# A fused attention, MLP and expert kernel on one core: splits, conversions and products moved between VectorE, ScalarE, GpSimd and TensorE

## The chip, the cores and the metric

The kernel runs on one core of a Trainium2 chip. Of its engines five matter here: TensorE (PE; its weight loads are listed apart as PEld), VectorE (DVE), ScalarE (ACT), GpSimd (POOL) and the queue of SyncE (SP) that issues the DMAs. Each engine takes its own instructions in order; semaphores tie them together. The metric is the device time of one execution in microseconds (us), the median of the runs shown.

## The reference

Three layers run one after the other. Inputs come in float32, the MLP's weights in float64.

```python
# 1. attention with random features, per head: 2 batches, 8 heads, 576 tokens, dimension 64, m = 128 features
q_s, k_s = q * scale, k * scale                      # scale = 64 ** -0.25
proj = x @ omega.T                                   # for k and for q
phi(x) = exp(proj - |x|^2/2 - rowmax(...)) / sqrt(m)
out = (phi(q) @ (phi(k).T @ v)) / (phi(q) @ sum_s phi(k) + 1e-6)
# 2. MLP on 1152 tokens, d_model 512, d_ff 2048
h = x @ w_in ;  g = h * tanh(softplus(h)) ;  y = g @ w_out
# 3. experts: 8, capacity 288
logits = y @ w_gate ; expert = argmax ; gate = softmax(logits)[expert]
position of a token = count of earlier tokens of its expert ; keep = position < capacity
out[i] = keep * gate * relu(y[i] @ w1[e]) @ w2[e]
```

## The kernel before

**Split numbers.** Most matmuls are done in float32r, a rounded form of float32. Each operand is cut into a high part (the rounded number) and a low part (the rest): `split_hi_lo` issues one copy or cast for the high part and one subtraction for the low part, each on an engine that the caller names. `mm3` then issues three matmuls (high x high, lines L67 to L69).

**Stage 1, attention (0 to 94 us).** Two heads make a pair, eight pairs in all. A pair has four or five tiles of 128 tokens. `beat` issues the work of one tile: `proj` (the projection, into a bank of PSUM `pj`), `phi` (on DVE the row maximum `mx`, L233, then `nm`, the maximum times minus the scale, L237; on ACT the exponential `e`, L242, and for q the shifted projection, L245), and beside it the previous pair's products: transposes `qt`, the sums `kvp`, and denominators and numerators `den` and `num` of two pairs. `split` cuts the k and q of a whole pair (1024 or 1280 columns) on POOL, two pairs ahead. The result x is split into `xh` and `xl`. A Tile scheduler orders this stage.

**Stage 2, first MLP layer (94 to 220.7 us).** The order here is the order of the program on each engine. The 2048 columns of `w_in` come in 16 chunks j. For each chunk `hmm(j, c)` makes a third c of the tokens: 12 matmuls of 384 columns into one of three banks `pj`. `hout` copies the bank to `g` (L430), on DVE for c = 0 and 1, on ACT for most c = 2; the bank is free for the third product after it only then. `convert` turns float64 bits to float32 in three DVE steps of 512 columns (L110, L112, L114), for `w_in` (`wi` to `wif`), for `w_out` (`wo` to `wl`) and for a transposed copy of `w_out` that the host lays out (`wt` to `woT`). `w_in`'s two parts `wih` and `wil` are made on POOL (L59, L63). The activation `mish` takes two chunks at a time in alternating ScalarE tables: in an even chunk a table load, tanh, sigmoid, tanh, sigmoid, and in an odd one a table load and two logarithms (L465 to L469, 1152 columns each); the product g times tanh follows on POOL (L470). `wgate_u` and `wgate_s` make w_out x w_gate out of `woT` (tiles `wu`, `us`, `ws`), from which `logits` gets the routing's logits `lg`.

**Stage 3, y of the first 288 tokens, and routing (220.7 to 262.1 us).** `ymm(ps0, j)` is 12 matmuls of 288 columns for each chunk of `w_out`, whose parts `whi`, `wl` and those of `g`, `gh`, are made two or three chunks ahead. Beside it run the last activations, the logits and `route0` to `route2`, a chain of small DVE steps and three matmuls `rp` with running sums `cu`.

**Stage 4 (262.1 to 349.9 us).** y of a second group of tokens, two experts' two layers each, and the output.

In stage 1, `phi` before the change:

```python
V.tensor_reduce(out=mx, in_=pv, op=ALU.max, axis=AX.X)
...
V.tensor_tensor(out=nm, in0=mx, in1=sgn, op=ALU.mult)
shift = p < 2 and t in (1, 3)
if shift:
    V.tensor_tensor(out=e[:, 2:4, :], in0=pv[:, 2:4, :], in1=mx[:, 2:4, None].to_broadcast([128, 2, M]), op=ALU.subtract)
for j in range(2):
    S.activation(out=e[:, j, :], in_=pv[:, j, :], func=AF.Exp, scale=SCALE, bias=nm[:, j : j + 1])
```

Of the kernel before, what the change touches and what calls it, by code (L numbers as in the profile page):

```python
# [32 lines left out]
def performer_mish_moe(  # L33
# [7 lines left out]
    w_outT: bass.AP,  # L41
# [12 lines left out]
    def split_hi_lo(src, hi, lo, eng_hi="act", eng_lo="pool"):  # L54
        """hi = src rounded to float32r, lo = src - hi (exact in float32r)."""
        if eng_hi == "act":
            S.copy(out=hi, in_=src)  # L57
        elif eng_hi == "pool":
            P.tensor_scalar(out=hi, in0=src, scalar1=1.0, scalar2=0.0, op0=ALU.mult, op1=ALU.add)  # L59
        else:  # L60
            V.tensor_copy(out=hi, in_=src)
        e = P if eng_lo == "pool" else V
        e.tensor_tensor(out=lo, in0=src, in1=hi.bitcast(F32), op=ALU.subtract)  # L63

    def mm3(o, lh, ll, rh, rl, start, stop):
        """o += (lh + ll)^T (rh + rl), without the product of the low parts' last bits."""
# [4 lines left out]
    # ---------------------------------------------------------------- constants  # L71
# [12 lines left out]
    # the eight PSUM banks: pj x 3, qt x 2, b0, b1, b2  # L84
# [13 lines left out]
    # w_in chunks for the float64 conversion: in flight while the attention runs  # L98
    fhl = tc.alloc_tile_pool(name="fhl", bufs=3)
# [7 lines left out]
    def conv64(t, dst):  # L107
        """float64 bit patterns to float32 (all bits that fit) in three steps; zero, or in float32's normal range."""
# [7 lines left out]
    win, wo, woT, raw = {}, {}, {}, {}  # L116

    def fetch(kind, j):
        src = dict(wi=w_in, wo=w_out, wt=w_outT)[kind]
# [27 lines left out]
    def finish(*gens):  # L147
        """what is left of each generator"""
# [4 lines left out]
    def steps(*gens):  # L153
        """four steps of each generator, in turn"""
# [3 lines left out]
    def hmm(j, c):  # L158
        """x @ w_in for a chunk of d_ff and a third of the tokens"""
# [7 lines left out]
    # ---------------------------------------------------------------- attention  # L167
    # phi's term |x|^2/2 is the same for all features of a row, so it cancels
    # against the row maximum; 1/sqrt(m) is carried by EPS.
    with ExitStack() as c2:  # L170
        a1 = c2.enter_context(tc.tile_pool(name="a1", bufs=1))
        omf = a1.tile([128, 2 * M], F32, name="omf")
        nc.sync.dma_start(out=omf, in_=omt)
# [5 lines left out]
        # the tensor engine's clock rises while the first operands are on their way  # L179
# [3 lines left out]
        for _ in range(8):  # L183
            T.matmul(out=wp, lhsT=wb[:, 0:128], rhs=wb, start=True, stop=True)
        split_hi_lo(omf, omh, oml, "dve", "dve")
# [21 lines left out]
        def halves(p):  # L207
            """the engines of the pieces' high and low parts"""
            return (("act", "dve"),) * 3 if p == 0 else (("act", "pool"),) * 2 if p == 1 else (("pool", "pool"),)

        def split(p):
# [3 lines left out]
            for c, e in zip(pieces(p), halves(p)):  # L215
# [3 lines left out]
        def proj(p, t):  # L219
            d = st[p]  # L220
            # the first pairs find the other banks empty
            first = {(0, 3): "b1", (1, 0): "b2", (1, 3): "b1", (1, 4): "b2"}
            d["p", t] = ps = bank(first.get((p, t), "pj"), "pj")
            for i in range(2):
                s = slice(256 * t + 128 * i, 256 * t + 128 * i + 128)
                mm3(ps[:, i * 256 : i * 256 + 256], d["h"][:, s], d["l"][:, s], omh, oml, True, True)

        def phi(p, t):
            """phi's exponents of a tile of tokens: exp for k, the shifted projection for q"""
            d = st[p]  # L230
            pv = d.pop(("p", t)).rearrange("p (g m) -> p g m", m=M)
            mx = a3.tile([128, 4], F32, name="mx", tag=f"mx{t}")
# [3 lines left out]
            nm = a3.tile([128, 4], F32, name="nm", tag=f"nm{t}")  # L236
            V.tensor_tensor(out=nm, in0=mx, in1=sgn, op=ALU.mult)  # L237
            shift = p < 2 and t in (1, 3)
            if shift:
                V.tensor_tensor(out=e[:, 2:4, :], in0=pv[:, 2:4, :], in1=mx[:, 2:4, None].to_broadcast([128, 2, M]), op=ALU.subtract)  # L240
            for j in range(2):
                S.activation(out=e[:, j, :], in_=pv[:, j, :], func=AF.Exp, scale=SCALE, bias=nm[:, j : j + 1])  # L242
# [4 lines left out]
        def kvm(p, h):  # L247
            """kv and, in the last column, the sum of phi(k) over the tokens: one accumulation for two pairs"""
# [9 lines left out]
        def kvc(u):  # L258
            """kv, and the sum of phi(k) in 32 equal columns"""
# [7 lines left out]
        def qtr(p, h):  # L267
# [21 lines left out]
        def den(u):  # L289
            """-1 / (the denominators), the same in the 32 rows of a head: a first value and a step of Newton's"""  # L290
# [17 lines left out]
        def num(u, k, last=False):  # L308
            """x^T for one half of the four heads' dimensions"""
# [12 lines left out]
            split_hi_lo(x, xh[:, e + k, c], xl[:, e + k, c], *(("act", "dve") if last else ("pool", "pool")))  # L322
# [27 lines left out]
        def beat(i, t, *pe):  # L350
            """a tile of pair i beside the tensor engine's other work, and the rest of what the last beat began"""
# [648 lines left out]
```

## Time and profile before

| | us |
|---|---|
| median of 3 runs (351.24, 352.63, 354.53) | 352.63 |
| span of the profiled execution, first to last instruction | 349.9 |
| median less that span | 2.7 |
| PE busy | 314.4 (90%) |
| DVE busy | 265.7 (76%) |
| ACT busy | 191.4 (55%) |
| POOL busy | 153.2 (44%) |

Matmuls overlap each other, so a busy PE is not yet a PE at its pace: the time from one matmul's start to the next one's is what it costs. The granted clock is the share of TensorE's full clock (2.4 GHz) that a stretch got; 0.50 is the lower of its two levels (1.2 GHz).

### The profile page before, as it was taken

The numbers are of one execution on the slowest core, as the hardware profiler recorded it, in microseconds if no ns is written. First come the engines' busy times: TensorE is split into PE (matmuls) and PEld (weight loads), VectorE is DVE, ScalarE is ACT, GpSimd is POOL, SyncE is SP. The second block draws the span as 40 slices with busy tenths as digits, with TensorE's granted clock in tenths as the row PEclk, the third lists the DMA queues.
The fourth block names the chain that finished last, engine by engine and source line by source line (L and its number), as shares of the span: only waits on it lengthen the run. The fifth ranks groups of instructions, "written<-read, shape, count | busy, mean of one in ns | idle before, by whom it ended". The sixth has DMA issues, their size and how long they took to land.

```text
span 349.9 us, 5915 instructions
## 1 busy us (share of the span) xinstructions
PE 314.4 (90%) x2159; PEld 281.1 (80%) x2160; DVE 265.7 (76%) x453; ACT 191.4 (55%) x375; POOL 153.2 (44%) x107
## 2 busy tenths in 40 slices
PE   8869988999999959699879989999599999999992
PEld 5758666767899959569875888677599999999992
DVE  5986999974789999987999999998935447324321
ACT  4657566697128736566554849584324663515411
POOL 2866693504064837556463711376610443241400
PEclk9988999999999969899969999999879999999998
DMA  7764724130075536397727350000004554650111
GB/s 220 264 228 159 283 62 171 44 123 2 0 207 214 185 127 233 105 325 262 226 97 235 102 182 0 2 1 2 0 0 165 167 153 141 189 153 22 48 36 40
DMA packets 20370, 45.28 MB, mean 129 GB/s; under 512 B 1808, under 2 KB 7632, under 8 KB 20336
## 3 DMA queue, kind: packets, MB, share of 16 engines
q1 hardware_dynamic: 20336, 44.84, 39.3%
q8 instruction: 19, 0.31, 0.4%
q14 instruction: 15, 0.12, 0.1%
HBM read 41.30 MB, written 3.54 MB: 128 GB/s over the span
## 4 chain that ended last, share of the span: by engine, by line
PE 49%; DVE 43%; issue 3%; ACT 1%; DMA 1%; POOL 1%; SPq 0%; POOLq 0%; ACTq 0%; DVEq 0%
PE py L67 6%; PE py L69 6%; PE py L68 6%; DVE nm L237 5%; PE h L67 4%; PE h L69 4%; PE h L68 4%; DVE woT L112 4%; DVE mx L233 3%; DVE wl L110 3%; DVE g L430 3%; DVE gh L63 3%; DVE wif L110 3%; DVE g L470 2%; DVE wif L112 2%
## 5 line engine op out<-in xcount | busy, mean ns | idle before, releaser
L63 POOL TENSOR_TENSOR wl<-wl,whi 128x512 fp32r<-128x512 f32 x32 | 44.4, 1391 | 84.1 <-ACT whi L57 44.0
L67 PE MATMUL h<-xh,wih 128*128 128x384 f32 x192 | 68.8, 358 | 12.3 <-DVE g L430 12.3
L68 PE MATMUL h<-xl,wih 128*128 128x384 f32 x192 | 67.1, 350 | 0.0
L69 PE MATMUL h<-xh,wil 128*128 128x384 f32 x192 | 67.1, 350 | 0.0
L67 PEld LDWEIGHTS h<-xh,wih 128*128 128x128 f32 x192 | 38.2, 199 | 19.5 <-DVE g L430 10.2
L59 POOL TENSOR_SCALAR wih<-wif 128x512 fp32r<-128x512 f32 x16 | 14.4, 898 | 64.6 <-PE h L68 23.2
L67 PE MATMUL py<-gh,whi 128*128 128x288 f32 x128 | 39.7, 310 | 0.8 <-DVE g L430 0.8
L68 PE MATMUL py<-gh,whi 128*128 128x288 f32 x128 | 39.1, 305 | 0.2 <-DVE gh L63 0.2
L69 PE MATMUL py<-gh,wl 128*128 128x288 f32 x128 | 39.0, 305 | 0.0
L69 PEld LDWEIGHTS h<-xh,wil 128*128 128x128 f32 x192 | 38.2, 199 | 0.5 <-issue 0.5
L68 PEld LDWEIGHTS h<-xl,wih 128*128 128x128 f32 x192 | 38.2, 199 | 0.0
L63 DVE TENSOR_TENSOR gh<-g,gh 128x288 fp32r<-128x288 f32 x32 | 23.2, 729 | 12.9 <-ACT gh L57 12.7
L242 ACT ACTIVATE e<-pj,nm 128x128 f32<-128x128 f32 x72 | 22.7, 376 | 18.8 <-DVE nm L237 16.7
L470 POOL TENSOR_TENSOR g<-g,em 128x1152 f32<-128x1152 f32 x10 | 29.1, 2928 | 2.4 <-ACT em L469 2.4
L67 PEld LDWEIGHTS py<-gh,whi 128*128 128x128 f32 x128 | 25.2, 197 | 6.0 <-issue 4.3
L233 DVE TENSOR_REDUCE mx<-pj 128x4 f32<-128x512 f32 x36 | 24.0, 680 | 6.8 <-PE pj L69 6.8
L465 ACT ACTIVATE em<-g 128x1152 f32<-128x1152 f32 x16 | 18.5, 1162 | 17.6 <-POOL g L470 7.7
L67 PE MATMUL pj<-omh,kqh 128*128 128x256 f32 x72 | 23.9, 333 | 2.1 <-ACT e L245 1.9
L68 PEld LDWEIGHTS py<-gh,whi 128*128 128x128 f32 x128 | 25.2, 197 | 0.6 <-DVE gh L63 0.6
L69 PEld LDWEIGHTS py<-gh,wl 128*128 128x128 f32 x128 | 25.2, 197 | 0.0
L63 POOL TENSOR_TENSOR wil<-wif,wih 128x512 fp32r<-128x512 f32 x16 | 24.6, 1540 | 1.3
L57 ACT CAST whi<-wl 128x512 fp32r<-128x512 f32 x41 | 24.2, 616 | 1.0 <-PE py L68 0.8
(160 smaller groups left out, 820.9 us busy)
## 6 DMA issues: line engine op xcount, KB each, us to landing
wi<-w_in SPq DMA_DIRECT2D x16, 512.0 KB, 4.3
wt<-w_outT SPq DMA_DIRECT2D x16, 512.0 KB, 4.3
wo<-w_out SPq DMA_DIRECT2D x16, 512.0 KB, 3.3
wl<-w SPq DMA_DIRECT2D x32, 256.0 KB, 2.8
out<-zero SPq DMA_DIRECT2D x1, 2304.0 KB, 11.3
kqf<-kq SPq DMA_DIRECT2D x3, 640.0 KB, 4.0
v<-va SPq DMA_DIRECT2D x4, 390.0 KB, 4.0
kqf<-kq SPq DMA_DIRECT2D x3, 512.0 KB, 3.7
```

The source lines that it names most:

```text
L57: S.copy(out=hi, in_=src)
L63: e.tensor_tensor(out=lo, in0=src, in1=hi.bitcast(F32), op=ALU.subtract)
L67: T.matmul(out=o, lhsT=lh, rhs=rh, start=start, stop=False)
L68: T.matmul(out=o, lhsT=lh, rhs=rl, start=False, stop=False)
L69: T.matmul(out=o, lhsT=ll, rhs=rh, start=False, stop=stop)
L110: V.tensor_scalar(out=a, in0=w[:, :, 1], scalar1=3, scalar2=0x3FFFFFF8, op0=ALU.logical_shift_left, op1=ALU.bitwise_and)
L112: V.scalar_tensor_tensor(out=a, in0=w[:, :, 1], scalar=-0x40000000, in1=a, op0=ALU.bitwise_and, op1=ALU.bitwise_or)
L233: V.tensor_reduce(out=mx, in_=pv, op=ALU.max, axis=AX.X)
L237: V.tensor_tensor(out=nm, in0=mx, in1=sgn, op=ALU.mult)
L242: S.activation(out=e[:, j, :], in_=pv[:, j, :], func=AF.Exp, scale=SCALE, bias=nm[:, j : j + 1])
L465: S.activation(out=em[j], in_=hv, func=AF.Sigmoid, scale=-1.0)
L470: eng.tensor_tensor(out=hv, in0=hv, in1=em.pop(j), op=ALU.mult)
```

## The change

In words, by stage:
- Attention: the scale goes into omega; the row maximum is written negated, so the step `nm` (a multiplication) is gone; the shift of q is a DVE step in every odd tile; POOL splits one tile of 256 columns at a time, and x in halves of 288; the first tile's projection is two float32 matmuls without a split; omega is loaded from ACT's queue; five warm-up matmuls in place of eight; the conversions that ran here are three chunks of `w_in`, beside pairs 6 and 7.
- First MLP layer: the transposed copy of `w_out` is no longer loaded (16 DMAs of 512 KB) or converted (16 x 3 DVE steps); `wturn` transposes each converted chunk on TensorE, four 128 x 128 transposes, and ACT copies the bank out. `wih` is cast on ACT, `wil` subtracted on DVE, all products of `mish` are on DVE: POOL issues nothing in this stage.
- Second part and routing: `ymm`'s first splits are all on DVE, later ones on ACT and POOL; `route0` is shorter; the running sums are eleven small matmuls instead of DVE steps; the gates are computed later.

```diff
         def convert(kind, j):
...
-            split_hi_lo(f, hi.rearrange("p a b -> p (a b)"), lo.rearrange("p a b -> p (a b)"), "pool")
+            split_hi_lo(f, hi.rearrange("p a b -> p (a b)"), lo.rearrange("p a b -> p (a b)"), "act", "dve")
             win[j] = (hi, lo)
-        elif kind == "wt":
-            woT[j] = h2.tile([128, 512], F32, name="woT", tag="woT", bufs=4)
-            yield from conv64(t, woT[j])
...
+            cut = pieces(p)[p == 0 :] if p < 2 else [slice(c, c + 256) for c in range(0, 1280 if p % 2 else 1024, 256)]
+            for c, e in zip(cut, halves(p)):
...
+                if (p, t) == (0, 0):
+
+                    T.matmul(out=ps[:, i * 256 : i * 256 + 256], lhsT=d["f"][:, s], rhs=oms, start=True, stop=True)
+                    continue
...
-            V.tensor_reduce(out=mx, in_=pv, op=ALU.max, axis=AX.X)
+            d["max"] = V.tensor_reduce(out=nm, in_=pv, op=ALU.max, axis=AX.X, negate=True)
...
-            V.tensor_tensor(out=nm, in0=mx, in1=sgn, op=ALU.mult)
-            shift = p < 2 and t in (1, 3)
+            shift = t % 2 == 1
             if shift:
-                V.tensor_tensor(out=e[:, 2:4, :], in0=pv[:, 2:4, :], in1=mx[:, 2:4, None].to_broadcast([128, 2, M]), op=ALU.subtract)
+                V.tensor_tensor(out=e[:, 2:4, :], in0=pv[:, 2:4, :], in1=nm[:, 2:4, None].to_broadcast([128, 2, M]), op=ALU.add)
...
+        def wturn(j):
+            b, i = divmod(j, 4)
+            if i == 0:
+                woT[b] = h2.tile([128, KT, 512], F32, name="woT", tag="woT", bufs=1)
+            u = bank("qt", "wt")
+            for k in range(KT):
+                T.transpose(u[:, k * 128 : k * 128 + 128], wo[j][:, k * 128 : k * 128 + 128], ident)
+            S.copy(out=woT[b][:, :, i * 128 : i * 128 + 128], in_=u.rearrange("p (k m) -> p k m", k=KT))
...
-                    eng.tensor_tensor(out=hv, in0=hv, in1=em.pop(j), op=ALU.mult)
+                if step in ("t", "tp"):
+                    V.tensor_tensor(out=hv, in0=hv, in1=em.pop(j), op=ALU.mult)
...
-        order = "ioioti", "ott", "i"
+        order = "ioi", "oi", "oi"
...
+            for k in range(1, NTT):
+                T.matmul(out=p[:TT, k * E : 96], lhsT=onesb, rhs=fl(R["oh"])[:, 0 : 96 - k * E], start=False, stop=(k == NTT - 1))
```

How the instructions stand. First VectorE in the attention, at pairs 1 and 2: `mx` is the maximum of a tile, `nm` what ACT takes as its bias, `e` the shifted q. Before:

```order
L233 TENSOR_REDUCE mx<-pj 128x4
L237 TENSOR_TENSOR nm<-mx,sgn 128x4
L240 TENSOR_TENSOR e<-pj,mx 128x256
L237 TENSOR_TENSOR nm<-mx,sgn 128x4
L233 TENSOR_REDUCE mx<-pj 128x4
L237 TENSOR_TENSOR nm<-mx,sgn 128x4
```

and after:

```order
L243 TENSOR_TENSOR e<-pj,nm 128x256
L238 TENSOR_REDUCE nm<-pj 128x4 x3
L243 TENSOR_TENSOR e<-pj,nm 128x256
L238 TENSOR_REDUCE nm<-pj 128x4 x2
L243 TENSOR_TENSOR e<-pj,nm 128x256
```

The multiplications that stood between the reductions are gone, and nothing else came between them. Next VectorE in an even chunk of the MLP, from the chunk's first `hout`: chunk 6 before (its tile of two chunks is `g_1290`), chunk 8 after (`g_1224`; `g_1222` is that of chunks 4 and 5). `wi`, `wo` and `wt` are the raw chunks as loaded. Before:

```order
L430 COPY g_1290<-h 128x384
L110 TENSOR_SCALAR wif<-wi_1607 128x512
L110 TENSOR_SCALAR wl<-wo_1609 128x512
L112 SCALAR_TENSOR_TENSOR wif<-wi_1607,wif 128x512
L112 SCALAR_TENSOR_TENSOR wl<-wo_1609,wl 128x512
L110 TENSOR_SCALAR woT<-wt_1611 128x512
L114 SCALAR_TENSOR_TENSOR wif<-wi_1607,wif 128x512
L430 COPY g_1290<-h 128x384
L114 SCALAR_TENSOR_TENSOR wl<-wo_1609,wl 128x512
L112 SCALAR_TENSOR_TENSOR woT<-wt_1611,woT 128x512
L114 SCALAR_TENSOR_TENSOR woT<-wt_1611,woT 128x512
```

and after:

```order
L438 COPY g_1224<-h 128x384
L488 TENSOR_TENSOR g_1222<-g_1222,em 128x1152 x2
L110 TENSOR_SCALAR wif<-wi_1701 128x512
L110 TENSOR_SCALAR wl<-wo_1703 128x512
L112 SCALAR_TENSOR_TENSOR wif<-wi_1701,wif 128x512
L438 COPY g_1224<-h 128x384
L112 SCALAR_TENSOR_TENSOR wl<-wo_1703,wl 128x512
L114 SCALAR_TENSOR_TENSOR wif<-wi_1701,wif 128x512
L114 SCALAR_TENSOR_TENSOR wl<-wo_1703,wl 128x512
L62 TENSOR_TENSOR wil<-wif,wih 128x512
```

The three `woT` steps left; two products (for the two chunks 4 and 5, in even chunks only) and the subtraction `wil` came, and the second `hout` now stands behind the products. Last ScalarE, an odd and an even chunk. Before:

```order
L457 ACT_TABLE_LOAD
L467 ACTIVATE em<-em,tiny 128x1152 x2
L440 COPY us<-wu 128x512
L430 COPY g_1290<-h 128x384
L457 ACT_TABLE_LOAD
L469 ACTIVATE em<-em 128x1152
L465 ACTIVATE em<-g_1290 128x1152
L469 ACTIVATE em<-em 128x1152
L465 ACTIVATE em<-g_1290 128x1152
L430 COPY g_1291<-h 128x384
```

and after:

```order
L474 ACT_TABLE_LOAD
L484 ACTIVATE em<-em,tiny 128x1152 x2
L438 COPY g_1223<-h 128x384
L450 COPY woT<-wt 128x4x128
L56 CAST wih<-wif 128x512
L474 ACT_TABLE_LOAD
L486 ACTIVATE em<-em 128x1152
L482 ACTIVATE em<-g_1223 128x1152
L486 ACTIVATE em<-em 128x1152
L482 ACTIVATE em<-g_1223 128x1152
L457 COPY us<-wu 128x512
L438 COPY g_1224<-h 128x384
```

Each chunk got two more ScalarE steps, the copy of the transposes and the cast `wih`, both behind the chunk's activations.

## Rows read from the trace of the kernel before

**Rows 1.** The windows view, one row for each stage (start-up, attention, first MLP layer, y of the first group with the routing, tail): start and end, length, then busy us and number of instructions of PE, PEld, DVE, ACT and POOL, the mean granted clock of TensorE, the DMAs' share and GB/s.

```profile
0.00:13.30 13.30, 10.77 (x61) 8.10 (x62) 9.49 (x25) 7.36 (x20) 6.08 (x11) 1.00 0.74 242
13.30:94.00 80.70, 73.27 (x609) 58.94 (x610) 66.98 (x122) 52.80 (x170) 40.90 (x29) 0.96 0.37 129
94.00:220.70 126.70, 114.16 (x637) 102.95 (x636) 120.10 (x165) 76.06 (x74) 63.13 (x37) 0.93 0.53 173
220.70:262.10 41.40, 35.30 (x252) 30.86 (x252) 33.53 (x74) 19.05 (x31) 21.87 (x15) 0.92 0.00 1
262.10:349.90 87.80, 80.95 (x610) 80.21 (x608) 35.56 (x69) 36.16 (x82) 21.25 (x16) 0.98 0.37 111
```

**Rows 2.** What TensorE waits for, by stage: three rows of the attention, one of the first MLP layer, three of the y stage. Waiting line, engine and line waited for: us in total, times, longest.

```profile
PE qt L275 <- ACT e L245: 3.2, 3, 1.7
PE pj L67 <- ACT e L245: 1.9, 4, 0.9
PE kvp L256 <- ACT e L242: 1.6, 2, 1.4
...
PE h L67 <- DVE g L430: 12.3, 6, 3.5
...
PE rp L674 <- DVE cu L664: 3.6, 1, 3.6
PE lg L476 <- DVE g L470: 1.5, 1, 1.5
PE py L67 <- DVE g L430: 0.8, 1, 0.8
```

**Rows 3.** The windows view again, three stretches of 6 us; the clock stands behind the five engines.

```profile
126.00:132.00 6.00, 5.65 (x18) 5.66 (x19) 5.97 (x10) 0.00 (x0) 2.19 (x2) 0.50 0.70 213
200.00:206.00 6.00, 3.80 (x20) 3.40 (x20) 5.93 (x10) 3.82 (x5) 2.23 (x2) 1.00 0.64 195
252.00:258.00 6.00, 5.70 (x25) 5.70 (x25) 1.76 (x8) 0.95 (x2) 1.28 (x1) 0.50 0.00 0
```

**Rows 4.** The groups of VectorE in the attention: line, engine, operation, output and input, count | busy us, mean ns of one | idle before it and what ended that.

```profile
L233 DVE TENSOR_REDUCE mx<-pj 128x4 f32<-128x512 f32 x31 | 20.8, 680 | 6.8 <-PE pj L69 6.8
L237 DVE TENSOR_TENSOR nm<-mx,sgn 128x4 f32<-128x4 f32 x32 | 20.6, 644 | 0.2
```

**Rows 5.** Timeline rows (start, length) of the multiplication `nm`, once without GpSimd's splits beside it and once with, and of the split beside it.

```profile
8.80 0.15 DVE L237 TENSOR_TENSOR nm<-mx,sgn 128x4 f32<-128x4 f32 x1
...
16.66 2.82 DVE L237 TENSOR_TENSOR nm<-mx,sgn 128x4 f32<-128x4 f32 x1
16.48 2.98 POOL L63 TENSOR_TENSOR kql<-kqf,kqh 128x1280 fp32r<-128x1280 f32 x1
```

**Rows 6.** Timeline rows of TensorE in the MLP layer: one `wu` group, then matmuls of `hmm` around four transposes `ws`, and one matmul behind a wait.

```profile
96.14 1.06 PE L438 MATMUL wu<-woT,wgf 128*32 128x512 f32 x8
...
101.08 0.33 PE L68 MATMUL h<-xl,wih 128*128 128x384 f32 x1
101.25 0.34 PE L69 MATMUL h<-xh,wil 128*128 128x384 f32 x1
101.43 0.60 PE L446 MATMUL ws<-cs,us 128*128 128x128 f32 x4
...
102.04 0.34 PE L68 MATMUL h<-xl,wih 128*128 128x384 f32 x1
...
126.35 0.69 PE L67 MATMUL h<-xh,wih 128*128 128x384 f32 x1 [3.51 <-DVE g L430]
```

**Rows 7.** Groups of the MLP layer (columns as in rows 4), the last one from the page's part 5, over the whole span.

```profile
L112 DVE SCALAR_TENSOR_TENSOR woT<-wt,woT 128x512 int32<-128x512 int32 x12 | 18.0, 1500 | 0.0
L114 DVE SCALAR_TENSOR_TENSOR woT<-wt,woT 128x512 int32<-128x512 int32 x12 | 10.9, 910 | 0.4
L110 DVE TENSOR_SCALAR woT<-wt 128x512 int32<-128x512 int32 x12 | 5.0, 419 | 0.2 <-DMA wt<-w_outT 0.2
L430 DVE COPY g<-h 128x384 f32<-128x384 f32 x32 | 17.4, 549 | 3.0 <-PE h L69 3.0
L457 ACT ACT_TABLE_LOAD x15 | 19.2, 1283 | 0.3
...
L57 ACT CAST whi<-wl 128x512 fp32r<-128x512 f32 x41 | 24.2, 616 | 1.0 <-PE py L68 0.8
```

**Rows 8.** Timeline rows of the MLP layer: a product pair on GpSimd and a conversion step on VectorE beside it; conversion steps with GpSimd idle; a product pair on VectorE.

```profile
117.60 5.80 POOL L470 TENSOR_TENSOR g<-g,em 128x1152 f32<-128x1152 f32 x2 [0.84 <-ACT em L469]
118.42 2.45 DVE L110 TENSOR_SCALAR wif<-wi 128x512 int32<-128x512 int32 x1
...
167.64 0.42 DVE L110 TENSOR_SCALAR wif<-wi 128x512 int32<-128x512 int32 x1
...
168.31 0.68 DVE L112 SCALAR_TENSOR_TENSOR wif<-wi,wif 128x512 int32<-128x512 int32 x1
168.91 0.68 DVE L112 SCALAR_TENSOR_TENSOR wl<-wo,wl 128x512 int32<-128x512 int32 x1
...
209.24 2.62 DVE L470 TENSOR_TENSOR g<-g,em 128x1152 f32<-128x1152 f32 x2
```

**Rows 9.** Timeline rows of ScalarE at a table switch.

```profile
104.65 1.28 ACT L457 ACT_TABLE_LOAD   x1
105.94 1.17 ACT L465 ACTIVATE em<-g 128x1152 f32<-128x1152 f32 x1
```

More of the change, by code (lines that the diff above doesn't have):

```diff
@@ L114, in conv64 @@
         V.scalar_tensor_tensor(out=a, in0=w[:, :, 0], scalar=29, in1=a, op0=ALU.logical_shift_right, op1=ALU.bitwise_or)
-    win, wo, woT, raw = {}, {}, {}, {}
+    win, wo, raw = {}, {}, {}
     def fetch(kind, j):
-        src = dict(wi=w_in, wo=w_out, wt=w_outT)[kind]
+        src = dict(wi=w_in, wo=w_out)[kind]
         t = fpool.tile([128, 512], I64, name=kind + "64", tag="raw", bufs=4)
@@ L182, in performer_mish_moe @@
         wp = bank("b2", "wp")
-        for _ in range(8):
+        for _ in range(5):
             T.matmul(out=wp, lhsT=wb[:, 0:128], rhs=wb, start=True, stop=True)
-        split_hi_lo(omf, omh, oml, "dve", "dve")
+        oms = a1.tile([128, 2 * M], F32, name="oms")
+        V.tensor_scalar(out=oms, in0=omf, scalar1=SCALE, scalar2=None, op0=ALU.mult)
+        V.tensor_scalar(out=omh, in0=omf, scalar1=SCALE, scalar2=None, op0=ALU.mult)
+        V.scalar_tensor_tensor(out=oml, in0=omf, scalar=SCALE, in1=omh.bitcast(F32), op0=ALU.mult, op1=ALU.subtract)
         st = {}
@@ L275, in qtr @@
                     T.transpose(q[:, t * 128 : t * 128 + 128], e[t][:, 2 + h, :], ident)
-                S.activation(out=qT[:, p % 2, h, 0:512], in_=q, func=AF.Exp, scale=SCALE)
+                S.activation(out=qT[:, p % 2, h, 0:512], in_=q, func=AF.Exp)
             else:
@@ L279, in qtr @@
                     T.transpose(q[:, i * 128 : i * 128 + 128], e[4][:, 2 + i, :], ident)
-                S.activation(out=qT[:, :, :, 512:SEQ], in_=q[:, 0:256].rearrange("p (h r t) -> p r h t", h=2, r=2), func=AF.Exp, scale=SCALE)
+                S.activation(out=qT[:, :, :, 512:SEQ], in_=q[:, 0:256].rearrange("p (h r t) -> p r h t", h=2, r=2), func=AF.Exp)
         def heads(u, o, c, w, s):
@@ L321, in num @@
             c = slice(b * SEQ, b * SEQ + SEQ)
-            split_hi_lo(x, xh[:, e + k, c], xl[:, e + k, c], *(("act", "dve") if last else ("pool", "pool")))
+            if last:
+                split_hi_lo(x, xh[:, e + k, c], xl[:, e + k, c], "act", "dve")
+            else:
+                for i in range(2):
+                    s = slice(i * GT, i * GT + GT)
+                    t = slice(b * SEQ + i * GT, b * SEQ + i * GT + GT)
+                    split_hi_lo(x[:, s], xh[:, e + k, t], xl[:, e + k, t], "pool", "pool")
         eps = a1.tile([128, 1], F32, name="eps")
         V.memset(eps, EPS)
-        sgn = a1.tile([128, 4], F32, name="sgn")
-        V.memset(sgn[:, 0:2], -SCALE)
-        V.memset(sgn[:, 2:4], -1.0)
         load(0)
@@ L369, in performer_mish_moe @@
             a, u, odd = i - 1, (i - 3) // 2, i % 2 == 1
-            if i + 2 < NPAIR and i > 0:
-                finish(split(i + 2))
+            sp = split(i + 2) if i + 2 < NPAIR and i > 0 else iter(())
+            advance(sp)
             beat(i, 0, *([lambda: den(u) if odd else num(u, 1)] if u >= 0 else []))
@@ L457, in table, with mish @@
             nc.scalar.preload_act_table_set(name)
-        def mish(step, *js, eng=P):
+        def mish(step, *js):
             for j in js:
@@ L478, in performer_mish_moe @@
         chunk, ghl = {}, {}
+        all0 = slice(0, GT)
         def ring_tiles(k):
-            p = whA if k < 7 else whB
-            return p.tile([128, 512], F32R, name="whi", tag="whi"), ring(F32R)
+            if k < 6:
+                hi = fhl.tile([128, KT, 128], F32R, name="whi", tag="wil" if k % 2 else "wih").rearrange("p a b -> p (a b)")
+            else:
+                hi = (whA if k < 13 else whB).tile([128, 512], F32R, name="whi", tag="whi")
+            return hi, ring(F32R)
         def wo_split(j, ehi, elo):
@@ L582, in performer_mish_moe @@
         table("exp_and_others")
-        prep(2, slice(0, GT), "dve", "pool")
+        for j in range(3):
+            g_split(j, all0, "dve", "dve")
+        mish("tp", 13)
         logits(2)
+        wgate_u(3)
         ps0 = [bank(t, "py") for t in ("pj", "pj", "pj", "qt")]
@@ L735, in route2 @@
             R["wA"], R["wB"] = wA, wB
+            rem = small("rem", [1, 1])
+            V.tensor_reduce(out=rem, in_=cnt, op=ALU.add, axis=AX.X)
+            yield
+            V.tensor_tensor(out=rem, in0=rem, in1=m0[:, 0:1], op=ALU.subtract)
+            yield
+            V.tensor_tensor(out=ri[:, 3:4], in0=rem, in1=m1[:, 0:1], op=ALU.subtract)
+            yield
+            cnti = cpool.tile([1, G * E], I32, name="cnti")
+            V.tensor_copy(out=cnti, in_=cnt)
+            R["cnti"] = cnti
         def expert_load(e, n, c):
@@ L883, in performer_mish_moe @@
     r1.release()
+    fhl.release()
     h3.release()
```

192 lines of the change are left out of this document (76 added, 116 removed).

## The prediction

> **What bounds the kernel now.** First I read the windows by stage [rows 1]. The reader is to see two things in them. In the tail PE is busy 80.95 of 87.8 us, and the change issues the same work there. In the three stages ahead of it PE is busy 85 to 91% of the time too, but its mean granted clock is 0.96, 0.93 and 0.92. So PE's busy time contains slow matmuls, and there are waits on top. In the MLP layer the fullest engine is VectorE, 120.1 of 126.7 us.
>
> The second view is PE's waits by stage [rows 2]: 6.7 us on ScalarE in the attention, 12.3 us on `hout` in the MLP layer, 5.9 us on VectorE in the y stage. The third is the clock behind such a wait. The wait of 3.5 us ends at 126.35 us [rows 6]; from 126 to 132 us PE is then busy 5.65 of 6 us, but with 18 matmuls, at 0.50, the lower level (1.2 GHz). From 252 to 258 us, behind the 3.6 us on `cu`, it is 0.50 again. From 200 to 206 us PE is busy only 3.80 of 6 us, but in pieces, and its clock is 1.00 [rows 3]. [...] A long wait thus costs nearly twice.
>
> The fourth view is why VectorE is late. In the attention `nm`, on 128 x 4 numbers, takes 0.15 us alone and 2.82 us beside GpSimd's split, and averages 0.644 us over 32 [rows 4, 5]. In the MLP layer a conversion step of 0.42 us takes 2.45 us beside a product pair on GpSimd [rows 8]. So VectorE is full of work that GpSimd stretches.
>
> **Attention, 80.7 us.** Removed: 32 `nm`, 20.6 us of VectorE [rows 4], each on the path from a projection to its exponential, and the exponentials are what PE waits for. The scale moves into omega, at no cost: one small setup step instead of another. Added: the q shift in all odd tiles; VectorE has room, since 67.0 - 20.6 leaves 46.4 of 80.7 us [rows 1]. GpSimd's splits become five pieces per pair instead of one; its 40.9 us stay about as many, and each piece blocks VectorE for a shorter time. What the stage loses now: 6.7 us of waits [rows 2] and 0.04 x 80.7 = 3.2 us of clock [rows 1], 9.9, with some tenths of smaller waits. I take a gain of 10.0, that is, nearly all. Bounds: 4, if the reductions are stretched by GpSimd as `nm` was (the waits fall by half, the clock stays down); 14, if PE also loses its gaps, 80.7 - 73.3 = 7.4 us of idle [rows 1], most of them, and the clock.
>
> Start-up (13.3 us): fewer warm-up matmuls, a first tile without split. DMAs are busy 0.74 of it at 242 GB/s [rows 1], and the bytes are the same; I take 0, between -1 and +1.
>
> **First MLP layer, 126.7 us.** What it loses now: 12.3 us of waits [rows 2] and, by the mean clock, up to 0.07 x 126.7 = 8.9 us [rows 1]; I take 7.5, since a part of the low clock falls into the waits. Together 19.8.
> Removed from VectorE: the 36 `woT` steps, 18.0 + 10.9 + 5.0 = 33.9 us [rows 7], and the stretching by GpSimd, which is empty here afterwards. New sum for VectorE, from durations without GpSimd: a step of L110 keeps 0.34 us of pace (167.64 to 168.31 holds two) and one of L112 or L114 0.60 [rows 8], so a converted chunk costs 0.34 + 2 x 0.60 = 1.54; 13 chunks of `w_in` and 16 of `w_out` make 44.7. Thirteen `wil`, two-input steps of the same width, by 0.68 [rows 8] 8.8; 34 `hout` by 0.549 [rows 7] 18.7; twelve products by 2.62/2 [rows 8] 15.7. With some 3 us of small steps: 91 us, of a layer of 116. VectorE stops being the bound.
> Added to ScalarE: 13 casts `wih` and 16 copies of transposes, by the 0.616 us of a 128 x 512 cast [rows 7] 17.9; 76.1 + 17.9 = 94 of 116 us.
> Added to PE: 16 x 4 transposes. Between 101.25 and 102.04 us four transposes and two steps of `hmm` of 0.17 us were done, so four cost 0.79 - 0.34 = 0.45 [rows 6]; 16 x 0.45 = 7.2 us, on the path, since PE is what is left as bound. One `wu` group of 1.06 us [rows 6] goes into the y stage.
> New waits: in an even chunk two products stand on VectorE ahead of the second `hout`. They wait for the last tanh, behind a table load of 1.28 us and the activations [rows 9]. Behind them are queued that `hout`, the chunk's conversion and `wil`, and PE's third product after it waits for the bank. I step this by hand: a pair of chunks wants about 14.6 us from ScalarE and VectorE in lockstep, and from PE 72 x 0.173 + 2 x 0.45 = 13.4 [rows 6]; some pairs lose up to 1 us, in short waits. I keep 3 us of the 19.8 as such stalls.
> Gain: 19.8 - 3 - 7.2 + 1.1 = 10.7. Bounds: 4, if half of the old losses stays; 15.4, if the idle 126.7 - 114.2 = 12.5 us [rows 1] goes, the clock stays at 1.00, and only the transposes are paid.
> A rule here: the Trainium skill, "ScalarE: Activation LUTs", section "What ACT_TABLE_LOAD costs", puts a table switch at 2.66 us, with about 1.38 us of drain ahead of the load. The row shows no drain: the load takes 1.28 us and the next activation starts 1.29 us after the load did [rows 9]. By the page ScalarE's sum would be, as an estimate, 94 + 15 x 1.38 = 115, level with the layer, and 2 x 1.38 = 2.8 us more for a pair of chunks, which is the first rival and more.
>
> **y stage and routing, 41.4 us.** What it loses: 5.9 us of waits [rows 2] and 0.08 x 41.4 = 3.3 of clock [rows 1], 9.2. The 3.6 us on `cu` are VectorE's running sums, eleven small matmuls now, some 0.7 us by 0.11 for each transpose [rows 6]; the 1.5 on the products end if the last products, now all on VectorE at 1.31 each, come earlier with the layer. Added: 0.7 and the `wu` group, 1.1. Gain 9.2 - 1.8 = 7.4. Bounds: 4 (the logits still wait, and the clock falls once) and 8.5 (the small matmuls lie in gaps).
>
> **Tail:** 0; it issues the same instructions.
>
> **Sum.** 10.0 + 10.7 + 7.4 = 28.1. Span 349.9 - 28.1 = 321.8; the median lies 2.7 above the profiled span, so **324 us** (324.5). All bounds at their good end give 349.9 - 37.9 - 1 + 2.7 = about 313; all at their bad end 349.9 - 12 + 1 + 2.7 = 341, but three at once are unlikely, and I stop at the dearer of the first two rivals, 338.
>
> **Rivals.**
> First, ScalarE and VectorE in lockstep bind the layer. For it: ScalarE is at 94 of 116 us, and the products sit between its tables. Against it: neither is above 82%. If each pair takes 16.4 us instead of 14.6, eight pairs cost 14 us more: layer 130, total 338.
> Second, the attention keeps its length, because ScalarE (52.8 us) or GpSimd (40.9) takes VectorE's place [rows 1]: 324 + 10 = 334. Against it: both are under 66%.
> Third, slower. The products on VectorE hold the second `hout` so long that PE waits 3.2 us or more in every pair, like the 3.5 us in the trace, and each wait drops the clock as it did there. The half clock then costs 18 matmuls (6.0/18 - 0.17 = 0.16 us each) 2.9 us [rows 3, 6]. Eight pairs by 3.2 + 2.9 make 49 us on a layer of 113 without stalls, 162 against my 116: total 370. [...] Against it: VectorE loses 34 us of work and all stretching.
> Fourth, the added transposes cost the clock. If each chunk's four make a third of its matmuls run at the lower level, 12 x 0.16 = 1.9 us, sixteen chunks lose 31 us and the time is 355, no change. The Trainium skill, "TensorE: Matmul & The Clock Gate", "Part 4: PE-mode transpose", says that transposes do not count as work for the full clock. Against it: the four at 101.43 us are followed by matmuls at the same 0.17 us pace [rows 6].
> That the change does not do what it says is no rival of size: the instructions move as shown.
>
> **How the numbers follow.** Forecast 0.80, first rival 0.08, second 0.07, third 0.03, fourth 0.02. The range is 313 to 338, as worked out above, with the first two rivals in it. A change of 1%, some 3.5 us, is about what a measurement of this kernel can tell from none. Faster by more: 0.95; within: 0.02; slower: 0.03.
>
> **What would show it.** Attention: no `nm`, PE's waits on `e` near 1 us, end near 84 us. Layer: VectorE at 87 to 92 us, no GpSimd, PE's waits on `g` under 1.5 us each, clock 1.00 throughout, end near 200. y stage: no wait on `cu`, end near 234. Span near 322. The forecast is wrong if PE's waits on `hout` stay above 3 us, if the clock falls behind the transposes, or if ScalarE's casts and copies (both ahead of the next table load) hold up tanh by more than the 1 us I allow a pair.

## The result, and the profile after

The changed kernel takes 317.75 us (median of 4 runs, 315.80 to 319.32); the kernel before took 351.94 beside it. The ratio is 0.903, with a 95% interval of 0.897 to 0.909. The prediction was 324 us, 313 to 338. Of the span, 349.9 became 317.2, so 32.7 us went where 28.1 had been forecast. The forecast of 324.5 was 6.7 us too long: 4.6 by the stages, and 2.2 because the median lay 2.7 above the profiled span before and 0.5 after.

The windows view of after, cut where the same instructions stand as in [rows 1] (the same matmul of `hmm`, of `ymm`), with the same columns:

```profile
0.00:13.30 13.30, 11.47 (x63) 9.18 (x65) 7.25 (x19) 7.80 (x22) 5.60 (x13) 1.00 0.76 255
13.30:84.60 71.30, 68.66 (x603) 56.49 (x602) 50.50 (x92) 47.22 (x146) 43.43 (x75) 0.95 0.35 114
84.60:196.40 111.80, 111.12 (x693) 103.33 (x695) 90.24 (x154) 89.01 (x102) 0.00 (x0) 1.00 0.41 139
196.40:229.80 33.40, 32.63 (x271) 28.59 (x271) 29.95 (x65) 21.23 (x36) 16.38 (x11) 1.00 0.08 25
229.80:317.20 87.40, 80.69 (x610) 79.94 (x608) 34.95 (x66) 36.13 (x82) 21.23 (x16) 0.98 0.34 102
```

The three middle stages went from 80.7, 126.7 and 41.4 us to 71.3, 111.8 and 33.4; start-up and tail kept their lengths within 0.4. In the MLP layer PE is busy 111.12 of 111.8 us at clock 1.00, and VectorE fell from 120.1 to 90.2. In the attention the mean clock is still 0.95.

What PE waits for, in the order attention, MLP layer (two rows), y stage; they answer to [rows 2]:

```profile
PE num L290 <- DVE t L307: 2.6, 1, 2.6
...
PE h L66 <- DVE g L438: 0.4, 1, 0.4
PE wt L449 <- DVE wl L114: 0.3, 1, 0.3
...
PE py L67 <- DVE gh L62: 0.8, 2, 0.6
```

The waits on `e`, on `cu` and on the logits' product are gone, and what is left of the waits on `hout` (L438) is one of 0.4 us. One wait of size is new, 2.6 us in the attention. The timeline at that place, of VectorE, of GpSimd, and PE's matmuls behind the wait:

```profile
42.60 0.41 DVE L243 TENSOR_TENSOR e<-pj,nm 128x256 f32<-128x256 f32 x1
42.93 3.99 DVE L309 SCALAR_TENSOR_TENSOR r<-t,r 128x288 f32<-128x288 f32 x1
46.84 0.44 DVE L307 SCALAR_TENSOR_TENSOR t<-den,r 128x288 f32<-128x288 f32 x1
...
42.69 1.44 POOL L62 TENSOR_TENSOR kql<-kqf,kqh 128x256 fp32r<-128x256 f32 x2
44.10 0.78 POOL L58 TENSOR_SCALAR kqh<-kqf 128x256 fp32r<-128x256 f32 x2
44.84 1.40 POOL L62 TENSOR_TENSOR kql<-kqf,kqh 128x256 fp32r<-128x256 f32 x2
46.21 0.40 POOL L58 TENSOR_SCALAR kqh<-kqf 128x256 fp32r<-128x256 f32 x1
46.70 0.82 POOL L62 TENSOR_TENSOR kql<-kqf,kqh 128x256 fp32r<-128x256 f32 x1
...
47.43 0.79 PE L290 MATMUL num<-qT,kv 128*32 128x288 f32 x8 [2.64 <-DVE t L307]
...
48.15 0.58 PE L66 MATMUL pj<-omh,kqh 128*128 128x256 f32 x1
```

The windows view of the stretch behind it:

```profile
48.15:55.50 7.35, 7.35 (x46) 6.30 (x43) 3.73 (x9) 3.70 (x13) 2.45 (x4) 0.55 0.20 57
```

The Newton step `r` (L309), with both operands and its result in SBUF, lasts 3.99 us while GpSimd runs its pieces without a gap; it ends at 46.92, behind the first one (46.61 to 46.70). The step `t` (L307) behind it reads PSUM and takes 0.44 us beside the same pieces. So the cause that was read for `nm` before sits in another instruction now, and the clock falls behind its wait too. The experiments begin there.

### The profile page after: what moved, and what is told of

It reads as the page before. It is cut to its first block, busy times and chain, and to the rows that moved or that the text cites. A ratio compares the mean times of both kernels' runs of the same rounds, so it can differ in the third digit from the quotient of the medians.

```text
span 317.2 us, 5932 instructions
## 1 busy us (share of the span) xinstructions
PE 304.6 (96%) x2228; PEld 277.5 (87%) x2229; DVE 212.9 (67%) x394; ACT 201.4 (63%) x385; POOL 86.6 (27%) x114
## 4 chain that ended last, share of the span: by engine, by line
PE 82%; DVE 10%; ACT 3%; DMA 1%; issue 1%; POOL 0%; DVEq 0%; SPq 0%; POOLq 0%; ACTq 0%
PE h L66 10%; PE h L67 10%; PE h L68 9%; PE py L67 6%; PE py L66 6%; PE py L68 6%; PE kvp L257 4%; PE pj L66 3%; PE num L290 3%; PE lg L494 3%; PE pj L68 2%; PE pj L67 2%; DVE gh L62 2%; PE qt L278 2%; PE ph L66 2%; PE ph L68 2%
## 5 line engine op out<-in xcount | busy, mean ns | idle before, releaser
L62 POOL TENSOR_TENSOR wl<-wl,whi 128x512 fp32r<-128x512 f32 x27 | 37.6, 1405 | 184.3 <-ACT whi L56 167.2
L66 PE MATMUL h<-xh,wih 128*128 128x384 f32 x192 | 66.6, 347 | 0.4 <-DVE g L438 0.4
L67 PE MATMUL h<-xl,wih 128*128 128x384 f32 x192 | 64.6, 336 | 0.0
L68 PE MATMUL h<-xh,wil 128*128 128x384 f32 x192 | 64.6, 336 | 0.0
L67 PE MATMUL py<-gh,whi 128*128 128x288 f32 x128 | 38.0, 297 | 0.8 <-DVE gh L62 0.8
L66 PE MATMUL py<-gh,whi 128*128 128x288 f32 x128 | 38.3, 300 | 0.0
L238 DVE TENSOR_REDUCE nm<-pj 128x4 f32<-128x512 f32 x36 | 24.4, 687 | 16.5 <-PE pj L68 16.5
L488 DVE TENSOR_TENSOR g<-g,em 128x1152 f32<-128x1152 f32 x16 | 21.6, 1356 | 14.0 <-ACT em L486 14.0
L62 POOL TENSOR_TENSOR kql<-kqf,kqh 128x256 fp32r<-128x256 f32 (+2 forms) x29 | 22.7, 798 | 7.4 <-ACT kqh L56 7.2
L62 DVE TENSOR_TENSOR wl<-wl,whi 128x512 fp32r<-128x512 f32 x21 | 16.5, 787 | 8.6 <-PE py L68 3.6
L56 ACT CAST gh<-g 128x288 fp32r (+1 forms) x27 | 11.7, 433 | 16.3 <-PE py L68 15.0
```

Source lines behind the costliest of these rows:

```text
L66: T.matmul(out=o, lhsT=lh, rhs=rh, start=start, stop=False)
L67: T.matmul(out=o, lhsT=lh, rhs=rl, start=False, stop=False)
L68: T.matmul(out=o, lhsT=ll, rhs=rh, start=False, stop=stop)
L238: d["max"] = V.tensor_reduce(out=nm, in_=pv, op=ALU.max, axis=AX.X, negate=True)
L488: V.tensor_tensor(out=hv, in0=hv, in1=em.pop(j), op=ALU.mult)
```

## The experiments

Each kernel was timed beside the kernel before. For the stages I compare the profiled executions by the point where the 37th matmul of `hmm` starts (the end of the attention: 94.0 us before, 84.6 after), and by the lengths of the stages behind it.

**r_psum.**

```diff
-            t = [a2.tile([128, GT], F32, name="t", tag="t") for c in range(2)]
+            t = o
```

> The changed kernel, where the first of the two Newton steps of the denominators writes its result t over the PSUM bank it read, so that the second step (r, L309) reads one operand from PSUM; nothing else is changed. Theory: r took 3.99 us once because both of its operands and its result lie in SBUF while GpSimd's splits run back to back; with one operand in PSUM it takes 0.45 us as L307 does, PE's wait of 2.64 us on it goes, and the half clock behind it (7.35 us at 0.55) too: 2.6 + 3.3 = 5.9 us less, about 312 us. Rival: r waits for GpSimd in another way (or for ScalarE's result), whatever its operands: 318 us, r still up to 4 us.

312.63 us (312.49 to 313.06), as the theory said, and faster than both kernels. The group of `r`:

```profile
L309 DVE SCALAR_TENSOR_TENSOR r<-den,r 128x288 f32<-128x288 f32 x8 | 3.5, 449 | 0.0
```

and the windows view of the attention:

```profile
13.30:78.40 65.10, 65.10 (x597) 53.18 (x597) 46.45 (x90) 46.65 (x145) 43.39 (x76) 1.00 0.36 122
```

`r` takes 0.449 us in the mean, PE has no gap left, the clock is 1.00 and the attention ends at 78.4 us. Nothing but the place of the tile `t` was changed, and four of the eight `r` still stand beside GpSimd's splits, each 0.447 or 0.448 us long. GpSimd does not slow VectorE as such; it slows steps whose operands all lie in SBUF.

**b_no_nm** (with the scale moved into omega, as in the change):

```diff
-            V.tensor_reduce(out=mx, in_=pv, op=ALU.max, axis=AX.X)
+            V.tensor_reduce(out=nm, in_=pv, op=ALU.max, axis=AX.X, negate=True)
...
-            V.tensor_tensor(out=nm, in0=mx, in1=sgn, op=ALU.mult)
```

> The kernel before with the step nm alone taken out (scale moved into omega, maximum written negated); splits on GpSimd stay one piece for each pair. Theory (the prediction's term): nm stretched by GpSimd is what ScalarE and then PE wait for, the attention becomes about 10 us shorter: 342 us. Rival: the other VectorE steps with all operands in SBUF (r, conversions) take the stretching over, and the gain needs the smaller pieces too: above 348 us.

349.56 us against 351.37, ratio 0.996 (0.992 to 1.000); the attention ends at 91.5 us. The rival was right. PE's waits in the attention:

```profile
PE num L286 <- DVE t L303: 5.8, 2, 4.5
PE pj L67 <- DVE nm L234: 0.9, 1, 0.9
```

The timeline of VectorE and GpSimd ahead of the longest:

```profile
27.65 1.65 DVE L112 SCALAR_TENSOR_TENSOR wif<-wi,wif 128x512 int32<-128x512 int32 x1
29.34 3.25 DVE L114 SCALAR_TENSOR_TENSOR wif<-wi,wif 128x512 int32<-128x512 int32 x1
32.51 0.81 DVE L303 SCALAR_TENSOR_TENSOR t<-den,r 128x288 f32<-128x288 f32 x2
33.24 1.89 DVE L305 SCALAR_TENSOR_TENSOR r<-t,r 128x288 f32<-128x288 f32 x2
...
28.71 3.33 POOL L63 TENSOR_TENSOR kql<-kqf,kqh 128x1280 fp32r<-128x1280 f32 x1
```

The waits on `e` are gone, as forecast, but the scheduler now puts conversion steps beside the split. L114, of a form that takes 0.68 us alone [rows 8], takes 3.25, and the Newton steps queued behind it make PE wait 4.5 us.

**a_nm_back** and **a_split_whole** undo one part each of the changed kernel, **a_nm_whole** both.

```diff
+            d["max"] = V.tensor_reduce(out=mx, in_=pv, op=ALU.max, axis=AX.X)
...
-            d["max"] = V.tensor_reduce(out=nm, in_=pv, op=ALU.max, axis=AX.X, negate=True)
...
+            V.tensor_tensor(out=nm, in0=mx, in1=sgn, op=ALU.mult)
```

> The changed kernel with the step nm put back (a multiplication by -1 on 128x4 numbers behind each maximum). Theory: it is stretched beside GpSimd's pieces, to about 0.5 us in the mean, ScalarE and PE wait again, and the clock falls once or twice more: 6 to 10 us more, about 325 us. Rival: beside pieces of 0.4 to 0.8 us the step stays near 0.2 us and hides: 318 to 319 us.

```diff
-            cut = pieces(p)[p == 0 :] if p < 2 else [slice(c, c + 256) for c in range(0, 1280 if p % 2 else 1024, 256)]
+            cut = pieces(p)[p == 0 :]
```

> The changed kernel with GpSimd's splits of k and q in one piece for each pair, as before. Theory: without nm few VectorE steps of the attention have all operands in SBUF (eight r, the conversions), so longer pieces cost little: 318 to 321 us. Rival: the small pieces are what the attention gained by: 326 us or more.

> The changed kernel with both undone: nm put back, and GpSimd's splits in one piece for each pair. Theory: nm is dear only beside long pieces (alone, put back, it cost 0.6 us; long pieces alone cost nothing), so both together bring back the waits of before: attention near 90 us, total 323 us or more. Rival: the attention gained by something else (the q shift off ScalarE, conversions moved out): 313 to 318 us.

318.35, 312.53 and 321.24 us; the attention ends at 83.8, 78.0 and 87.4. The group of `nm` in a_nm_back:

```profile
L242 DVE TENSOR_TENSOR nm<-mx,sgn 128x4 f32<-128x4 f32 x32 | 8.5, 273 | 0.3
```

The same in a_nm_whole:

```profile
L242 DVE TENSOR_TENSOR nm<-mx,sgn 128x4 f32<-128x4 f32 x32 | 17.4, 550 | 0.3
```

The group of `r` in a_split_whole:

```profile
L309 DVE SCALAR_TENSOR_TENSOR r<-t,r 128x288 f32<-128x288 f32 x8 | 4.7, 596 | 0.0
```

`nm` costs 0.273 us in the mean beside small pieces and 0.550 beside whole ones. With whole pieces its removal is worth 87.4 - 78.0 = 9.4 us of attention. I had expected whole pieces alone to cost 0 to 3 us; they gained 5, as much as r_psum: with them `r` lasts 1.12 us at the longest (mean 0.596), and PE does not wait on it. In a_nm_back `r` averages 0.577, and PE's wait on it is gone too; what replaces it lies in the first 12 us, where two `nm` of 0.88 and 1.38 us stand beside GpSimd's first splits (PE's waits there):

```profile
PE kvp L259 <- ACT e L247: 1.3, 1, 1.3
PE qt L280 <- DVE e L245: 1.0, 1, 1.0
```

The mean clock of the first 13.3 us is 0.92, and the time stays that of after, as the rival had it. a_nm_whole, at 321.24, falls between its theory (323 or more) and its rival (313 to 318).

**b_no_nm_rp**: b_no_nm with the edit of r_psum.

> The kernel before without nm, and with the Newton step r reading PSUM as in the earlier run. Theory: taking nm out alone gained only 1.8 us because r, the next VectorE step with all operands in SBUF, was stretched to over 4 us twice beside GpSimd's long pieces and PE waited 5.8 us for it, the clock falling behind; with r out of the way the attention ends near 81 to 83 us instead of 91.5, total about 341 us. Rival: another step takes the stretching over again: 348 us.

348.71 us, attention to 89.2. The expectation misread b_no_nm: the longest `r` there lasted 1.52 us and not over 4; most of the wait came from the conversion ahead of it. The rival was right again: the waits are now on whatever is queued behind a stretched conversion. The timeline of VectorE, then of PE:

```profile
28.81 3.27 DVE L114 SCALAR_TENSOR_TENSOR wif<-wi,wif 128x512 int32<-128x512 int32 x1
32.00 0.82 DVE L303 SCALAR_TENSOR_TENSOR den<-den,r 128x288 f32<-128x288 f32 x2
32.73 0.81 DVE L305 SCALAR_TENSOR_TENSOR r<-den,r 128x288 f32<-128x288 f32 x2
...
33.23 2.15 PE L286 MATMUL num<-qT,kv 128*32 128x288 f32 x16 [3.92 <-DVE r L305]
```

So three kinds of step with all operands in SBUF stood beside the splits: `nm`, the conversions, `r`. The change took out the first and moved the second to pairs 6 and 7, where GpSimd no longer splits for a later pair. It left the third. Moving the conversions was not tried by itself.

**The MLP layer.** Three runs ask what made it shorter: the `woT` steps off VectorE, or GpSimd's absence.

**a_mul_pool.**

```diff
-                    V.tensor_tensor(out=hv, in0=hv, in1=em.pop(j), op=ALU.mult)
+                    (P if j < 10 else V).tensor_tensor(out=hv, in0=hv, in1=em.pop(j), op=ALU.mult)
```

> The changed kernel with the first ten products of the activation on GpSimd as before (2.9 us each there), six on VectorE. Theory: it is GpSimd beside VectorE that made the layer slow: the conversions of the chunks are stretched again (steps of 0.42 and 0.68 us to 2 us and more), PE waits for hout and the clock falls: the layer 5 to 15 us longer, about 327 us. Rival: it was the number of VectorE's steps; with ten products fewer VectorE is freer, PE stays the bound: 317 us.

**b_wturn** (the core of the edit; `wturn` is that of the diff above):

```diff
-        order = "ioioti", "ott", "i"
+        order = "ioi", "oi", "oi"
...
-                t=convert("wt", j + 1) if 3 <= j < NJ - 1 else iter(()),
...
+                if c == (1 if j == NJ - 1 else 2):
+                    wturn(j)
```

> The kernel before with one part of the change alone: the transposed copy of w_out is neither loaded nor converted, wturn makes it on TensorE and ScalarE copies it out. GpSimd still makes the products and w_in's two parts beside VectorE, nm is still there. Theory from the run with the products back on GpSimd (layer 111.8 us all the same): the 34 us of woT steps were what made VectorE the bound, stretching alone did not: the layer comes to 112 to 116 us, PE the bound, total about 338 us. Rival (stretching by products and wih, wil together fills VectorE without woT too): layer 120 us or more, 345 us.

**b_mul_dve.**

```diff
-        def mish(step, *js, eng=P):
+        def mish(step, *js, eng=V):
```

> The kernel before with all products of the activation on VectorE (ten of 2.9 us on GpSimd become ten of 1.3 us on VectorE); w_out is still converted twice. Theory: VectorE's stretching by the products goes (up to 2.5 us for a step of 0.42), which is more than the 13 us that the products add: 343 to 350 us. Rival: VectorE, already full at 120 of 126.7 us, gets 13 us more: 360 us or more.

315.89, 335.67 and 346.73 us. The windows view of the layer in a_mul_pool:

```profile
82.30:194.10 111.80, 111.12 (x693) 103.32 (x693) 96.72 (x144) 89.44 (x102) 29.22 (x10) 1.00 0.41 139
```

in b_wturn:

```profile
91.60:203.10 111.50, 110.98 (x693) 103.47 (x696) 98.79 (x128) 81.93 (x88) 63.66 (x37) 1.00 0.42 140
```

in b_mul_dve:

```profile
94.60:217.70 123.10, 112.77 (x637) 99.48 (x639) 113.52 (x175) 76.03 (x74) 32.78 (x27) 0.96 0.56 178
```

And a conversion group of a_mul_pool:

```profile
L114 DVE SCALAR_TENSOR_TENSOR wif<-wi,wif 128x512 int32<-128x512 int32 x13 | 21.3, 1638 | 0.0
```

In a_mul_pool conversion steps are stretched again, to 1.638 us in the mean, and the layer is 111.8 us all the same; my theory for it failed. In b_wturn GpSimd keeps 63.7 us of work in the layer, and the layer is 111.5. Taking the products off GpSimd alone gained 126.7 - 123.1 = 3.6 (b_mul_dve; its time, 0.985 of before with an interval of 0.978 to 0.992, lies in the range that I expected). Taking out the `woT` steps is enough for the layer's whole gain: without them VectorE is no longer full, stretched or not, and PE is the bound. Their loads went with them in b_wturn and are not priced apart; VectorE waited 2.9 us for DMAs in the layer before.

**a_wt_host.**

```diff
+        fetch("wt", 0)
+        order = "ioit", "oit", "oit"
...
+                t=convert("wt", j),
...
-                if c == (1 if j == NJ - 1 else 2):
-                    wturn(j)
```

> The changed kernel with the transposed w_out loaded and converted on VectorE as before (48 steps in the layer, 24.6 us more by 0.34 and 0.60), the transposes on TensorE and their ScalarE copies gone; GpSimd stays empty in the layer. By the sums VectorE has 90 + 25 = 115 us and PE 111.8 - 7.2 = 104.6. Theory (stretching was the larger part): the layer is bound by VectorE at 115 to 118 us, 4 to 6 us more: 323 us. Rival (the number of steps was the larger part): near the layer of before, 126 us, 332 us.

346.71 us, layer 137.9, worse than before. But in my placement PE waited 12.4 us in all for the last `woT` step ahead of `wu`, and VectorE 10.6 us for the loads, so the run says little on the two sums. It is inconclusive.

**a_turn2.**

```diff
-            for k in range(KT):
+            for k in [*range(KT), *range(KT)]:
                 T.transpose(u[:, k * 128 : k * 128 + 128], wo[j][:, k * 128 : k * 128 + 128], ident)
```

> The changed kernel with each chunk's four transposes of w_out done twice into the same bank: 64 transposes more, nothing else. Theory: they cost what was predicted for them, 0.45 us for four, 7.2 us: 325 us, clock 1.00 in the layer. Rival: transposes cost the clock: some 30 us more, clock under 0.9 in the layer. A third: they lie in gaps of PE: 318 us.

322.68 us. The layer:

```profile
81.70:200.10 118.40, 118.15 (x757) 110.29 (x760) 90.88 (x154) 90.24 (x103) 0.00 (x0) 1.00 0.39 132
```

It is 118.4 - 111.8 = 6.6 us longer, 0.41 for four transposes, at clock 1.00. (The total rose by 4.9, because the attention was shorter in these executions, 81.7; see the last section.) The Trainium skill's rule that transposes do not count as work for the clock ("TensorE: Matmul & The Clock Gate", "Part 4: PE-mode transpose") shows no effect here: 128 of them among the layer's matmuls left it at full speed.

**a_cu_dve** (the sums `cu` as in the kernel before, in place of the eleven matmuls):

```diff
-            for k in range(1, NTT):
-                T.matmul(out=p[:TT, k * E : 96], lhsT=onesb, rhs=fl(R["oh"])[:, 0 : 96 - k * E], start=False, stop=(k == NTT - 1))
+            T.matmul(out=p[:TT, 0:96], lhsT=onesb, rhs=fl(R["cu"]), start=False, stop=True)
```

> The changed kernel with the running sums of the routing as VectorE steps (nine small ones in one row, as before) instead of eleven small matmuls. Theory (the prediction's term): PE waits for them again, about 3.6 us, and runs at half clock behind that: 5 to 6.5 us more in the y stage, against after. Rival: beside ymm the sums have time, since the routing runs earlier now: 0 to 1 us.

320.49 us. The windows view of the y stage:

```profile
193.30:231.00 37.70, 33.51 (x262) 29.43 (x262) 30.81 (x76) 21.47 (x37) 15.42 (x11) 0.95 0.07 22
```

and what PE waits for in it:

```profile
PE py L67 <- DVE gh L62: 4.1, 1, 4.1
```

37.7 against 33.4 us. PE does not wait for the sums themselves now, but for a split `gh` queued behind them on VectorE. The term is 4.3 us, a little under the 5 to 6.5 expected, of the 8.0 that the stage gained. (The total rose by 2.7 only, because the attention ended at 81.5 here.) The other 3.7 us were not separated.

## Why the prediction was right

**The bound.** It was VectorE ahead of the tail, as read from [rows 1, 2], with the clock falling behind long waits [rows 3]. The profile after and r_psum show both: take the wait away, and the low clock goes with it. The clock does not fall behind long waits alone, though. In the attention before, no wait was above 1.7 us, and the rows are these:

```profile
19.00:22.80 3.80, 1.50 (x10) 1.17 (x10) 3.73 (x6) 1.76 (x6) 3.72 (x3) 1.00 0.72 261
22.80:29.60 6.80, 6.13 (x28) 6.13 (x29) 4.61 (x12) 5.43 (x18) 1.06 (x3) 0.50 0.15 61
```

Two waits, of 1.7 and 1.4 us, end at 20.45 and 23.47, and the clock is at its lower level (1.2 GHz) from 22.80 on. So short waits went with a low clock here, as they did not between 200 and 206 us [rows 3].

**Attention, forecast -10.0, measured -9.4.** The size was right by luck; the step that gave it was not whole. I put it all on `nm` [rows 4, 5], nothing on the rest of the stage's changes, and expected the smaller pieces to help. The windows view of a_nm_whole, then of a_split_whole:

```profile
13.30:87.40 74.10, 69.96 (x611) 55.62 (x610) 62.48 (x124) 47.71 (x149) 37.34 (x36) 1.00 0.33 109
13.30:78.00 64.70, 64.70 (x596) 52.93 (x595) 46.56 (x90) 46.36 (x144) 36.43 (x35) 1.00 0.36 122
```

With all of the change but these two parts (a_nm_whole) the stage ends at 87.4 instead of 94.0: 6.6 us from what I had put at nothing. `nm` then gives 9.4 (78.0), and the smaller pieces take back 6.6 (84.6), because `r` is held among them; in the medians these two are 8.7 and 5.2. That the sum of the three comes near 10.0 is a coincidence. Which part gave the first 6.6 is not separated; b_wturn, with four of the seven conversions and their loads out of the attention, and `nm` and whole pieces kept, ends it at 91.6, 2.4 us earlier than before. On the kernel before, `nm` alone gained 1.8 us in the median, with an interval that reaches to none, because conversions and `r` then hit the same splits. My lower bound of 4 was for reductions stretched in its place. The reductions read PSUM and were not stretched: 0.680 us before [rows 4], 0.682 to 0.689 in the runs. And I named no row for `r`.

**MLP layer, forecast -10.7, measured -14.9.** By my own sum the difference has three terms. The stalls that I kept at 3 us measured 0.7. The transposes measured 6.6, not 7.2. The losses of before were mis-sized: the layer's work without transposes and with the moved `wu` group is 111.8 - 0.7 - 6.6 + 1.1 = 105.6, so 21.1 us of the 126.7 had been lost where I took 19.8. VectorE's new sum, 91, measured 90.2; ScalarE's, 94, measured 89.0. What I had as the second reason, that GpSimd's absence frees VectorE, was true of the steps and worth nothing to the layer (a_mul_pool, b_wturn).

**y stage, forecast -7.4, measured -8.0; start-up and tail 0, measured 0 and -0.4.** The sums were the larger part (a_cu_dve, 4.3). In b_wturn `cu` stays, and the last products come 15.7 us earlier with the layer, but not earlier against it; PE still waits 3.6 us for `cu` and 1.4 for the logits' product. So an earlier layer alone does not end the second wait, as I had it. The changed kernel issues these products earlier among the chunks of `ymm`: they end 8.5 us after its first matmul, against 14.3 before and 15.3 in b_wturn.

**Slips in the sum.** Eleven small matmuls by 0.11 are 1.2 us where I wrote 0.7 (PE was busy with them for 0.62). The good ends of layer and y stage come to 15.3 and 8.1 by their own terms, where 15.4 and 8.5 stand. None of it moves the forecast or the range by much more than 1 us.

**The rivals.** Lockstep of ScalarE and VectorE: PE is busy 111.12 of 111.8 us. No drain shows at the table loads either, in after as in [rows 9] (timeline of ScalarE):

```profile
105.82 0.62 ACT L56 CAST wih<-wif 128x512 fp32r<-128x512 f32 x1
106.46 1.28 ACT L474 ACT_TABLE_LOAD   x1
107.75 1.16 ACT L486 ACTIVATE em<-em 128x1152 f32<-128x1152 f32 x1
```

The load starts 0.02 us after the cast ends, and tanh 1.29 after that, against the 2.66 us of the Trainium skill ("ScalarE: Activation LUTs", "What ACT_TABLE_LOAD costs"); the measurement decides. That section gives the drain's length and not its side; the row has room for it on neither. Attention unchanged and transposes at the cost of the clock did not happen. The slower case needed waits of 3.2 us on `hout`; the longest was 0.4.

## What to carry to other kernels

When a tiny step takes nearly twenty times its length, look at what else has all its operands in SBUF on that engine: take the one out, and the next stands in its place. Moving one operand to PSUM cured it with one line. Cutting the neighbour's work into small pieces did not cure it; it cost 5 us here. And where an engine is full beside a neighbour that slows it, ask first for less work: the layer's 14.9 us came with 34 us of steps removed, whether GpSimd was busy or not.

## What was new about the hardware

- VectorE steps with all operands in SBUF can be held while GpSimd's instructions follow each other: 3.99 us for a step of 0.45, ending only where GpSimd paused. Steps with an operand in PSUM are not (`t`, the reductions, `hout` at 0.553 us in a_mul_pool as in after). The Trainium skill ("SBUF — State Buffer", "Who interferes with whom") describes one pair of ports that VectorE and GpSimd share under an exclusive lock; the rows agree, and add that splitting GpSimd's work into pieces of 0.4 to 0.8 us doesn't help where the pieces stand back to back.
- After waits of nearly the same length at one place the clock fell in one execution and not in another. After 2.64 us in after it was 0.55 in the mean for 7.35 us. After 2.69 us at the same place in a_cu_dve the row is this, and the attention ended at 81.5 us instead of 84.6:

```profile
48.00:56.00 8.00, 8.00 (x78) 7.12 (x75) 6.40 (x14) 5.69 (x18) 5.32 (x8) 1.00 0.17 52
```

That is likely why the four runs of after fall near 316 and 319 us (mean clocks 0.996 and 0.991 against 0.984 and 0.984), while those of r_psum, without the wait, lie within 0.6; it was not tested by itself.
